# Up-projecting the last three token chunks by seven block products, in six PSUM banks

## The chip, the cores and the metric

The kernel runs on one core of a Trainium2 chip. Its engines work at the same time, each through its own queue of instructions in the order of the program: PE multiplies matrices (PEld is its loading of stationary blocks), DVE, ACT and POOL work on rows of up to 128 partitions, and SP and ACT issue transfers between the chip's memories. PE writes its results to PSUM, in which this kernel has eight banks of 128 x 512 fp32 numbers; DVE and ACT read them there. An instruction that needs another engine's result waits on a semaphore. The metric is the device time of one execution in microseconds (us); less is better.

## What is computed

The reference is attention with a sliding window followed by a two-layer network with a leaky ReLU:

```python
def _attn_ref(q, k, v):                      # (8, 8, 576, 64)
    ...
    mask_plain = (rel >= 0) & (rel < 32)
    mask_dil = (rel >= 0) & (rel < 128) & (rel % 4 == 0)
    masks = np.stack([mask_plain if h < H // 2 else mask_dil for h in range(H)], axis=0)
    ...
    return np.matmul(attn, v).astype(np.float32)

def _moe_ref(x, w_in, w_out):                # x (4608, 512), w_in (512, 2048), w_out (2048, 512)
    h = x @ w_in
    g = np.maximum(0.01 * h, h)
    return (g @ w_out).astype(np.float32)
```

The eight heads of a token, 64 numbers each, are laid side by side and make the 512 numbers of a row of x. The change is in h = x @ w_in.

## The kernel before, in words

**Tiling.** The 4608 tokens (8 batches of 576) are worked off in pairs of batches, m = 0 to 3. A pair's attention output stands transposed in `xt[m % 2]`, 128 partitions of the 512 features by 4 blocks (NI = 4) of 1152 tokens. A pair is cut into three chunks of 384 tokens, so there are 12 chunks, 0 to 11; chunks 9, 10 and 11 are those of the last pair. Within a pair each chunk is a set of columns of `xt`; `columns` (L514) gives their start and steps.

**Up-projection** (`up`, L997). The 2048 hidden numbers are 16 blocks of 128 (NJ = 16). For each chunk and each block j, four matmuls (L1014) accumulate over the features: a stationary block of `w_in` (128 x 128, every second column) against 384 moving columns of `xt`, into one of the two banks `hps`. One ACT instruction (L1025) then applies the leaky ReLU and writes the block to `gt[c % 3]` in fp16. So a chunk is 64 matmuls of 384 columns and 16 ACT instructions. One chunk of the first pair is done in two halves of 192 columns.

**Down-projection.** The first eight tiles of 128 tokens (PLAIN = 8) are projected plainly (`down`, L1055, matmuls L1066). The other 28 tiles are taken four at a time by `group` (L1105), which computes a product of 2 x 2 blocks with seven block products in place of eight: the four token tiles in two pairs are one side's blocks, and the hidden and output numbers, each cut in two, are the other's. Sums and differences of blocks of `gt` are formed by DVE (`add_up`, L1139), those of `w_out` once at about 75 us into the plan (`weight_sums`, L1091, DVE at L1095). Each product is 2 x 8 matmuls of 256 columns (L1153). Between products, ACT or DVE copies a bank's partial sums to SBUF (`evict`, L1182 and L1184), and DVE adds a bank to such a copy (`plus`, L1190). Products that build on each other accumulate in the same bank without clearing it, each after the eviction of what stood there.

A group can begin when the chunks of its tiles are up-projected. `tiles` is the list of (chunk, tile) in order, `groups` cuts it from the ninth tile on into fours. The last group is (10, 2), (11, 0), (11, 1), (11, 2) and is `split`: it uses six banks instead of two, every product is evicted in halves of 256 columns, and its results go to `v_all` and are stored half by half.

**Banks.** `sps0` and `tp` hold attention scores, the two `ops` attention outputs and transposes, the two `hps` the up-projection, the two `fps` the down-projection. The four of attention are free once the last batch's attention is done.

**Order.** All work is first entered as tasks with an engine (or a choice of engines), an assumed duration and a priority; `_Plan.run` (L85) then lays out the order of each engine's queue at build time. The order in the queue is fixed from then on: an instruction that waits holds up all behind it on its engine. `ring` (L281) hands out buffers in turn, with the users that must be done before one is reused. Priorities of the up-projection follow `begins`, 20.8 us per chunk (MOE).

**Stores** (`store`, L1049). `rows` (L1033) finds which output rows a tile's partitions belong to, in runs; each run is one transfer, issued on SP, or in the last group on SP and ACT in turn (line 263 is the helper that issues every transfer). An instruction that issues a transfer also waits until an older one, whose semaphore it takes over, has landed.

The lines by which the last group got its banks and its result buffers:

```python
            cells = [[(b, 0) for b in pair] for pair in (fps, [sps0, tpf], ops)]
            room.update({id(b): rings["S2"][-1] for b in (sps0, tpf)})
            room.update({id(b): sum(rings["O2"][-2:], []) for b in ops})
            ...
                r = (row + col) * 2 + pair[0]
                ob, o_old, o_users = v_all[:, r * HN:r * HN + HN], sum(rings["V2"][-NVS:], []), []
```

Of the kernel before, what the change touches and what calls it, by code (L numbers as in the profile page):

```python
# [11 lines left out]
AF = mybir.ActivationFunctionType  # L12
ALU = mybir.AluOpType
# [129 lines left out]
def kernel(  # L143
# [853 lines left out]
    def up(c, j, x, n, done, acc):  # L997
# [32 lines left out]
        acc[j].append((t_a, x, n))  # L1030
        return t_p

    def rows(c, tt):  # L1033

        m, i, _ = chunks[c]
        res = []
        for p in range(128):
            x = columns(c, tt * 128 + p, 1)[0]
            for b in (2 * m, 2 * m + 1):
                for u0, nu, base in segs[b]:  # L1040
                    if base <= x < base + 4 * nu:
                        tok = b * S + 4 * (u0 + (x - base) % nu) + (x - base) // nu
            if res and tok == res[-1][1] + 4 * res[-1][2]:
                res[-1][2] += 1
            else:
                res.append([p, tok, 1])
        return res

    def store(ob, i, c, tt, c0, n_o, t_c, users, both=False):  # L1049
        for n_p, (p0, tok, n) in enumerate(rows(c, tt)):  # L1050
            users.append(load("ACT" if both and n_p else "SP",
                              dram(out, tok * DM + c0, [4 * DM, n], [1, n_o]),
                              ob[p0:p0 + n, i:i + n_o], n, 4 * n_o, [t_c], -3000))

    def down(c, tt, acts, at_time):  # L1055

# [18 lines left out]
        f_users.append(t_c)  # L1075
        gt_free[c].extend(parts)
        plain_parts.extend(parts)
        store(ob, 0, c, tt, 0, DM, t_c, o_users)

    plain_parts = []  # L1080
    HJ, HN = NJ // 2, DM // 2
# [18 lines left out]
        minus(3, w_block(0, 1), w_block(1, 1), w_block(0, 1), [t_sum[1]] + plain_parts)  # L1100

    last_of = {}
    SUMS = 75.0

    def group(four, acts, at_time, split):  # L1105

# [11 lines left out]
                    for t, x, n_x in a if x < tt * 128 + 128 and x + n_x > tt * 128]  # L1118

        used = {i: [] for i in range(4)}  # L1120
        if split:
            cells = [[(b, 0) for b in pair] for pair in (fps, [sps0, tpf], ops)]
            pairs = ((0,), (1,))
            room = {id(b): last_of[id(b)] for b in fps}
            room.update({id(b): rings["S2"][-1] for b in (sps0, tpf)})
            room.update({id(b): sum(rings["O2"][-2:], []) for b in ops})
        else:
            cells = [[(b, HN * i) for i in range(2)] for b in (*fps, fps[1])]
            pairs = ((0, 1),)
            room = {id(b): last_of.get(id(b), first_banks.get(id(b), [])) for b in fps}  # L1130
# [61 lines left out]

        def result(make, deps, pair, row, col):
            if split:
                r = (row + col) * 2 + pair[0]
                ob, o_old, o_users = v_all[:, r * HN:r * HN + HN], sum(rings["V2"][-NVS:], []), []
            else:
                on, o_old = ring("OSB", NO, o_users := [])
                ob = osb[on]
            t = make(ob, deps + o_old)  # L1200
            for x, i in enumerate(pair):
                c, tt = four[row + i]
                store(ob, HN * x, c, tt, col * HN, HN, t, o_users, split)
            return t

        def kept_of(n, pair):
# [110 lines left out]
    for m in range(B // 2):  # L1317
# [97 lines left out]
```

## Time and profile before

| | |
|---|---|
| median of 3 runs | 309.73 us (309.62 to 309.89) |
| the profiled execution, its own time | 311.24 us |
| its span in the profile | 309.5 us |
| PE busy | 297.8 us, 96% of the span |
| DVE, ACT, POOL busy | 204.3, 178.7, 126.1 us |
| up-projection on PE, all 12 chunks (L1014) | 144.3 us busy, 812 matmuls recorded |
| leaky ReLU on ACT (L1025) | 93.7 us, 203 instructions |
| down-projection by groups on PE (L1153, the largest of its rows) | 53.6 us, 416 matmuls |
| share of the chain that ended last | PE 87%, DMA 4%, DVE 3%, issue of transfers on SP 3%, ACT 1% |

The span begins with the first instruction of the program and ends with its last one; the device time of that execution has a little more around it. "Busy" is the time in which an engine has an instruction under way. Matmuls overlap each other in PE's pipeline, so that the length of one is more than the time until the next one starts, and the same holds for queued instructions of DVE and ACT. The chain of work that ended last is followed back from the end: at each step to what released an instruction, or to the one before it on its engine. Lines are those of the kernel before.

### The profile page before, as it was taken

The numbers are of one execution on the slowest core, as the hardware profiler recorded it, in microseconds if no ns is written. First come the engines' busy times: TensorE is split into PE (matmuls) and PEld (weight loads), VectorE is DVE, ScalarE is ACT, GpSimd is POOL, SyncE is SP. The second block draws the span as 40 slices with busy tenths as digits, with TensorE's granted clock in tenths as the row PEclk, the third lists the DMA queues.
The fourth block names the chain that finished last, engine by engine and source line by source line (L and its number), as shares of the span: only waits on it lengthen the run. The fifth ranks groups of instructions, "written<-read, shape, count | busy, mean of one in ns | idle before, by whom it ended". The sixth has DMA issues, their size and how long they took to land.

```text
span 309.5 us, 7405 instructions
## 1 busy us (share of the span) xinstructions
PE 297.8 (96%) x2795; PEld 214.1 (69%) x2795; DVE 204.3 (66%) x419; ACT 178.7 (58%) x426; POOL 126.1 (41%) x178
## 2 busy tenths in 40 slices
PE   7987999999999999999999999999999999999993
PEld 2534645567777777787777878787887767777882
DVE  5854896689786859969798798967645230070551
ACT  3736775786556678465776665556545655445320
POOL 4449555475675639268645671961000000000000
PEclk9999999999999999999999999999999999999998
DMA  7999998999899999985999978793103010310133
GB/s 245 314 333 401 397 355 152 223 216 222 235 179 221 210 167 192 167 206 123 193 179 181 194 153 193 137 201 80 36 22 84 6 30 2 84 51 2 36 100 105
DMA packets 163188, 51.25 MB, mean 166 GB/s; under 512 B 140752, under 2 KB 160080, under 8 KB 163152
## 3 DMA queue, kind: packets, MB, share of 16 engines
q1 hardware_dynamic: 162128, 50.05, 68.1%
q10 hardware_dynamic: 1024, 0.73, 0.9%
q8 instruction: 22, 0.36, 0.5%
q14 instruction: 14, 0.11, 0.1%
HBM read 41.32 MB, written 9.44 MB: 164 GB/s over the span
## 4 chain that ended last, share of the span: by engine, by line
PE 87%; DMA 4%; DVE 3%; SPq 3%; ACT 1%; issue 1%; DVEq 0%; ACTq 0%
PE hps L1014 38%; PE fps L1153 25%; PE fps L1066 9%; PE ops L931 3%; DMA wst<-in_moe_w_in_dram 3%; SPq L263 3%; PE ops L979 2%; DVE ee L924 1%; DMA stg<-in_k_dram 1%; PE ops L1153 1%; PE tp L610 1%; PE sps L891 1%; PE tp L891 1%; PE sps L898 1%; PE tp L898 1%; ACT gt L1025 1%
## 5 line engine op out<-in xcount | busy, mean ns | idle before, releaser
L1014 PE MATMUL hps<-xt,w_in 128*128 128x384 f16 (+1 forms) x812 | 144.3, 313 | 1.4 <-DVE w_in L273 0.7
L1025 ACT ACTIVATE gt<-hps 128x384 f16<-128x384 f32 (+1 forms) x203 | 93.7, 468 | 69.9 <-PE hps L1014 67.9
L1014 PEld LDWEIGHTS <-w_in 128*128 128x128 f16 x832 | 75.2, 98 | 37.7 <-DVE w_in L273 1.5
L1153 PEld LDWEIGHTS <-gt 128*128 128x128 f16 x672 | 64.7, 98 | 12.0
L597 POOL COPY slots<-turned 64x576 f16<-64x576 f16 x48 | 35.5, 740 | 51.5 <-DVE turned L592 46.8
L1153 PE MATMUL fps<-w_out,gt 128*128 128x256 f16 x416 | 53.6, 273 | 0.0
L273 POOL CAST nat<-stg 128x576 f16<-128x576 f32 (+1 forms) x53 | 38.2, 745 | 7.5 <-DMA stg<-in_q_dram 2.7
L1066 PE MATMUL fps<-w_out,gt 128*128 128x512 f16 x128 | 32.4, 379 | 0.0
L1190 DVE TENSOR_TENSOR osb<-fps,stg 128x512 f32<-128x512 f32 x18 | 12.4, 688 | 28.0 <-ACT stg L1182 19.0
L953 DVE TENSOR_TENSOR rc<-ops,recs 96x384 f16<-96x384 f32 x48 | 25.8, 541 | 0.3
L1182 ACT COPY stg<-fps 128x512 f32<-128x512 f32 (+1 forms) x24 | 12.8, 532 | 13.2 <-PE fps L1153 11.8
L273 POOL CAST vd<-v_all 128x1024 f16<-128x1024 f32 (+2 forms) x20 | 18.0, 918 | 5.5 <-DMA v_all<-in_v_dram 5.3
L949 DVE RECIPROCAL recs<-ops 96x6 f32<-96x6 f32 x48 | 8.9, 185 | 17.2 <-PE ops L931 15.0
L924 DVE TENSOR_TENSOR ee<-ee,con 128x576 f16<-128x576 f16 x24 | 16.7, 699 | 3.8 <-ACT ee L910 3.7
L562 DVE COPY slots<-tp 64x128 f16<-64x128 f16 (+7 forms) x43 | 13.8, 334 | 8.0 <-PE tp L610 7.4
L592 DVE STREAM_TRANSPOSE turned<-nat 128x576 f16<-128x576 f16 x24 | 17.9, 755 | 0.0
L1066 PEld LDWEIGHTS <-gt 128*128 128x128 f16 x128 | 11.5, 98 | 9.1
L603 DVE STREAM_TRANSPOSE slots<-nat 128x576 f16<-128x576 f16 x24 | 17.6, 749 | 0.0
L924 DVE TENSOR_TENSOR el<-el,con 128x576 f16<-128x576 f16 x24 | 15.7, 656 | 2.1 <-ACT el L910 2.1
L273 POOL CAST vp<-v_all 128x768 f16<-128x768 f32 x16 | 15.4, 970 | 3.3 <-DMA v_all<-in_v_dram 2.1
L1139 DVE TENSOR_TENSOR gt<-gt 128x1024 f16<-128x1024 f16 x19 | 12.9, 692 | 3.8 <-PE fps L1153 3.7
L776 ACT ACTIVATE ee<-sps 128x384 f16<-128x384 f32 x20 | 9.8, 490 | 8.6 <-PE sps L770 5.7
(120 smaller groups left out, 399.6 us busy)
## 6 DMA issues: line engine op xcount, KB each, us to landing
stg<-in_q_dram SPq DMA_DIRECT2D x48, 144.0 KB, 3.8
stg<-in_k_dram SPq DMA_DIRECT2D x48, 144.0 KB, 2.9
v_all<-in_v_dram SPq DMA_DIRECT2D x24, 256.0 KB, 3.5
v_all<-in_v_dram SPq DMA_DIRECT2D x24, 192.0 KB, 2.9
gt<-in_moe_w_in_dram SPq DMA_DIRECT2D x5, 512.0 KB, 8.1
out_dram<-osb SPq DMA_DIRECT2D x24, 96.0 KB, 2.0
out_dram<-osb SPq DMA_DIRECT2D x36, 48.0 KB, 1.8
out_dram<-osb SPq DMA_DIRECT2D x25, 64.0 KB, 2.1
```

What stands on the lines that cost most here:

```text
L273: ENG[e].tensor_copy(out=dst, in_=src)
L562: nc.vector.tensor_copy(out=dst, in_=src)
L592: lambda e: nc.vector.transpose(xb, na[:, 0:S]), prio)
L597: lambda e, p0=p0, hh=hh: nc.gpsimd.tensor_copy(out=at(qb, p0, p0 + 64, hh * S + o, *od), in_=at(xb, p0, p0 + 64, i, *id_)), prio, 0.0, "m ...
L603: lambda e: nc.vector.transpose(kb[:, PAD:PAD + S], na[:, S:2 * S]), prio)
L924: nc.vector.tensor_tensor(out=x, in0=x, in1=mk, op=ALU.mult)
L953: nc.vector.tensor_tensor(out=at(xb, 0, 96, 768 * n + 64 * i, [256, 3], [128, 2], [1, D]), in0=at(ot, 0, 96, 0, [130, 3], [65, 2], [1, D]) ...
L1014: nc.tensor.matmul(ht[:, 0:n], at(w_in, 0, 128, i * DFF + j // 2 * 256 + j % 2, [2, 128]), at(xt[m % 2], 0, 128, i * 1152 + x0, *dims), st ...
L1025: lambda e: nc.scalar.activation(out=gt[c % NG][:, j * n_c + x:j * n_c + x + n], in_=ht[:, 0:n], func=AF.Prelu, alpha=0.01),
L1066: nc.tensor.matmul(ft, g[:, j * n_c + tt * 128:j * n_c + tt * 128 + 128], w_out[:, j * DM:j * DM + DM], start=(j == 0), stop=(j == NJ - 1))
L1139: lambda e: nc.vector.tensor_tensor(out=dst, in0=a, in1=b, op=op),
L1153: nc.tensor.matmul(bk[:, x:x + HN], tl[:, off + j * step:off + j * step + 128], rhs(j), start=first and x == 0 and j == 0, stop=j == HJ - ...
```

## The change

Chunks 9, 10 and 11 are up-projected by `up_fast` in place of `up`. The chunk's 384 tokens are cut in halves y of 192, the 512 features in halves k, the 2048 hidden numbers in halves h. The product of these 2 x 2 blocks is formed by seven block products. A `quarter` takes 2 of the 8 hidden blocks of 128 of each half; a chunk is four quarters. In a quarter, each product is four matmuls of 192 columns, two hidden blocks z by two feature blocks i, and fills 2 x 192 columns of a bank. Each quarter has a pair of banks X and Y: X takes products 1, 6, 5 and 3 one on top of the other, evicted after each of the first three; Y takes 2, then 7 afresh, then 4 on top of it. Three pairs are used in turn: the two `hps`, `sps0` with `tp`, and the two `ops`. Copies and sums are kept in `stg`, four tiles of three 384-column fp32 pieces. Four ACT instructions of 2 x 192 columns per quarter apply the leaky ReLU, three of them to the sums in `stg`, one to bank X, and write `gt` in the columns that `up` used too.

The operands that are sums are formed on DVE: four of `w_in` once (`w_in_sums`, 128 x 2048 fp16 each, three into the attention's `vd` tiles, the fourth in place over a block of `w_in`, after all plain projections), and four of `xt` for each chunk (`less`, 128 x 384 fp16, into a `vp` tile).

The tile (9, 2) is moved in `tiles` to the place before the last three. The last two groups become (9, 1), (10, 0), (10, 1), (10, 2) and (9, 2), (11, 0), (11, 1), (11, 2). In the last group, `sps0`, `tp` and `ops` are free when the last users of `up_ring` are done, and for the first pair of tiles both halves of a result, now side by side in `v_all`, are stored together in rows of 512 numbers: 12 stores where there were 18.

```diff
@@ -502,6 +502,7 @@
     MOE = 20.8
     PLAIN = 8
     tiles = [(c, tt) for c in range(len(chunks)) for tt in range(3)]
+    tiles.insert(-3, tiles.pop(-7))
     groups = [tiles[i:i + 4] for i in range(PLAIN, len(tiles), 4)]
     begins = [0.0]
     for m, x, n in chunks:
@@ -1030,6 +1031,138 @@
         acc[j].append((t_a, x, n))
         return t_p
 
+    plain_ups, w_in_sum, up_ring = [], {}, []
+    QJ = NJ // 2
+
+    def in_block(k, n):
+        return at(w_in, 0, 128, 2 * k * DFF + n * DFF // 2, [DFF, 2], [1, DFF // 2])
+
+    def w_in_sums():
+
+        def both(n, dst, x, y, op, deps):
+            w_in_sum[n] = add("DVE", 1.25, 0.2, deps, lambda e: nc.vector.tensor_tensor(
+                out=dst, in0=x, in1=y, op=op), IN_SUMS + n, 0.0, "T")
+
+        def home(i):
+            return at(vd[i], 0, 128, 0, [DFF // 2, 2], [1, DFF // 2])
+        v = rings["VD"]
+        last = {(len(v) - k) % NV: v[-k] for k in range(1, NV + 1)}
+        both(1, home(0), in_block(0, 1), in_block(1, 1), ALU.add, last[0])
+        both(2, home(1), home(0), in_block(0, 0), ALU.subtract, last[1] + [w_in_sum[1]])
+        both(4, home(2), in_block(1, 0), home(1), ALU.subtract, last[2] + [w_in_sum[2]])
+        both(3, in_block(0, 1), in_block(0, 0), in_block(0, 1), ALU.subtract,
+             [w_in_sum[1]] + plain_ups)
+
+    def up_fast(c, done, acc):
+
+        m, _, n_c = chunks[c]
+        n = n_c // 2
+        if not up_ring:
+            w_in_sums()
+            up_ring.append([[(hps[0], hps[1]), rings["H"][-1] + rings["H"][-2]],
+                            [(sps0, tpf), rings["S2"][-1]],
+                            [ops, rings["O2"][-1] + rings["O2"][-2]]])
+            up_ring.append([sum(rings["STG"][-NST:-1], []) + sum(rings["STG4"][1 - NST:], [])] * 4)
+        x_of = [columns(c, n * y, n)[0] for y in range(2)]
+        v = rings["VP"]
+        home, old = vp[len(v) % NV], v[-NV]
+        v.append([])
+        tx = {k: at(home, 0, 128, 2 * n * (k - 1), [n, 2], [1, n]) for k in range(1, 5)}
+        t_x = {}
+
+        def b(k, y):
+            return at(xt[m % 2], 0, 128, 2304 * k + x_of[y], [1152, 2], [1, n])
+
+        def less(k, x, y, deps):
+            t_x[k] = add("DVE", 0.08 + 2 * n * 0.00056, 0.2, deps, lambda e: nc.vector.tensor_tensor(
+                out=tx[k], in0=x, in1=y, op=ALU.subtract), begins[c] - 8, 0.0, "A")
+        less(1, b(0, 1), b(0, 0), done + old)
+        less(2, b(1, 1), tx[1], [t_x[1]])
+        less(3, b(1, 1), b(0, 1), done + old)
+        less(4, b(1, 0), tx[2], [t_x[2]])
+
+        def raw(k, h):
+            return lambda j, i: at(w_in, 0, 128, (2 * k + i) * DFF + h * DFF // 2 + j // 2 * 256 + j % 2,
+                                   [2, 128])
+
+        def summed(t):
+            return lambda j, i: at(vd[t], 0, 128, i * DFF // 2 + j // 2 * 256 + j % 2, [2, 128])
+
+        def x_raw(k, y):
+            return lambda i: at(xt[m % 2], 0, 128, (2 * k + i) * 1152 + x_of[y], [1, n])
+
+        def x_sum(k):
+            return lambda i: at(home, 0, 128, 2 * n * (k - 1) + n * i, [1, n])
+
+        w_all = sum((w_in_t[j] for j in range(NJ)), [])
+        g, g_old = gt[c % NG], gt_free.get(c - NG, [])
+
+        def quarter(p):
+            bank_of = up_ring[0].pop(0)
+            (X, Y), room = bank_of
+            room_k = up_ring[1].pop(0)
+            kn = (4 * (c - FAST[0]) + p) % 4
+            keep = [stg[kn][:, 2 * n * z:2 * n * z + 2 * n] for z in range(3)]
+            when = begins[c] + p * 4.6 - (0.0, 2.0, 7.0)[c - FAST[0]]
+
+            def product(k, lhs, rhs, cell, first, deps):
+                def pe(e):
+                    for z in range(2):
+                        for i in range(2):
+                            nc.tensor.matmul(cell[:, n * z:n * z + n], lhs(2 * p + z, i), rhs(i),
+                                             start=first and z == 0 and i == 0,
+                                             stop=z == 1 and i == 1, skip_group_check=True)
+                return add("PE", 0.33, 0.25, deps, pe, when + 0.6 * k, 0.0, "U")
+
+            def evict(z, deps):
+                dst = keep[z]
+
...
+                return add((("ACT", 0.5), ("DVE", 0.55)), None,
+                           0.22, deps, fn, -1000 + c * 16, 0.0, "C")
+
+            def plus(z, deps):
+                return add("DVE", 0.09 + 2 * n * 0.00115, 0.25, deps, lambda e: nc.vector.tensor_tensor(
+                    out=keep[z], in0=Y[:, 0:2 * n], in1=keep[z], op=ALU.add), -1000 + c * 16, 0.0, "C")
+
+            def relu(src, row, y, deps):
+                j = row * QJ + 2 * p
+                t = add("ACT", 0.45, 0.22, deps + g_old,
+                        lambda e: nc.scalar.activation(
+                            out=at(g, 0, 128, j * n_c + n * y, [n_c, 2], [1, n]),
+                            in_=at(src, 0, 128, 0, [n, 2], [1, n]), func=AF.Prelu, alpha=0.01),
+                        -1000 + c * 16 + p)
+                for z in range(2):
+                    acc[j + z].append((t, n * y, n))
+                return t
+
+            p1 = product(0, raw(0, 0), x_raw(0, 0), X, True, done + w_all + room)
+            p2 = product(1, raw(1, 0), x_raw(1, 0), Y, True, done + w_all + room)
+            e1 = evict(0, [p1] + room_k)
+            a11 = plus(0, [e1, p2])
+            r11 = relu(keep[0], 0, 0, [a11])
+            p6 = product(2, summed(1), x_sum(2), X, False, [e1, t_x[2], w_in_sum[2]])
+            p7 = product(3, raw(0, 1), x_sum(3), Y, True, [a11, t_x[3], w_in_sum[3]])
+            e2 = evict(1, [p6] + room_k)
+            p5 = product(4, summed(0), x_sum(1), X, False, [e2, t_x[1], w_in_sum[1]])
+            e4 = evict(2, [p5] + room_k)
+            a22 = plus(2, [e4, p7])
+            r22 = relu(keep[2], 1, 1, [a22])
+            p3 = product(5, summed(2), x_raw(1, 1), X, False, [e4, w_in_sum[4]])
+            p4 = product(6, raw(1, 1), x_sum(4), Y, False, [a22, t_x[4]])
+            r12 = relu(X[:, 0:2 * n], 0, 1, [p3])
+            a21 = plus(1, [e2, p4])
+            r21 = relu(keep[1], 1, 0, [a21])
+            up_ring[0].append([bank_of[0], [r12, a21]])
+            up_ring[1].append([r11, r22, r21])
+
+        for p in range(QJ // 2):
+            quarter(p)
+
     def rows(c, tt):
 
         m, i, _ = chunks[c]
...
@@ -1100,7 +1233,8 @@
         minus(3, w_block(0, 1), w_block(1, 1), w_block(0, 1), [t_sum[1]] + plain_parts)
 
     last_of = {}
-    SUMS = 75.0
+    SUMS, IN_SUMS = 75.0, 190.0
+    FAST = (9, 10, 11)
 
     def group(four, acts, at_time, split):
 
@@ -1118,12 +1252,13 @@
                     for t, x, n_x in a if x < tt * 128 + 128 and x + n_x > tt * 128]
 
         used = {i: [] for i in range(4)}
+        whole = {i: [] for i in range(4)}
         if split:
             cells = [[(b, 0) for b in pair] for pair in (fps, [sps0, tpf], ops)]
             pairs = ((0,), (1,))
             room = {id(b): last_of[id(b)] for b in fps}
-            room.update({id(b): rings["S2"][-1] for b in (sps0, tpf)})
-            room.update({id(b): sum(rings["O2"][-2:], []) for b in ops})
+            for pair, users in up_ring[0]:
+                room.update({id(b): users for b in pair})
         else:
             cells = [[(b, HN * i) for i in range(2)] for b in (*fps, fps[1])]
             pairs = ((0, 1),)
@@ -1192,15 +1327,23 @@
 
         def result(make, deps, pair, row, col):
             if split:
-                r = (row + col) * 2 + pair[0]
-                ob, o_old, o_users = v_all[:, r * HN:r * HN + HN], sum(rings["V2"][-NVS:], []), []
+                r = 2 * (row + pair[0]) + col
+                ob, o_old = v_all[:, r * HN:r * HN + HN], sum(rings["V2"][-NVS:], [])
+                t = make(ob, deps + o_old)
+                whole[row + pair[0]].append(t)
+                at_once = len(whole[row + pair[0]]) if row == 0 else 1
+                if row or at_once == 2:
+                    c, tt = four[row + pair[0]]
+                    store(v_all, r * HN - (at_once - 1) * HN, c, tt, (col + 1 - at_once) * HN,
+                          at_once * HN, whole[row + pair[0]][-at_once:], [], True)
+                return t
             else:
                 on, o_old = ring("OSB", NO, o_users := [])
                 ob = osb[on]
             t = make(ob, deps + o_old)
             for x, i in enumerate(pair):
                 c, tt = four[row + i]
-                store(ob, HN * x, c, tt, col * HN, HN, t, o_users, split)
+                store(ob, HN * x, c, tt, col * HN, HN, [t], o_users)
             return t
 
         def kept_of(n, pair):
@@ -1333,8 +1476,12 @@
             acts = first_acts if n_c == 0 else [[] for _ in range(NJ)]
             halves = [(0, 192), (192, 192)] if m == 0 and n_c % 3 == 2 else [(0, 384)]
             for i, (x, n) in enumerate(halves):
-                x_free[m + 2] += [up(n_c, j, x, n, x_done[n_c, i], acts)
-                                 for j in range(0 if n_c else N_UPS, NJ)]
+                if n_c in FAST:
+                    up_fast(n_c, x_done[n_c, i], acts)
+                    continue
+                plain_ups += [up(n_c, j, x, n, x_done[n_c, i], acts)
+                              for j in range(0 if n_c else N_UPS, NJ)]
+                x_free[m + 2] += plain_ups[-(NJ if n_c else NJ - N_UPS):]
             gt_free[n_c] = []
             all_acts[n_c] = acts
             for i, (c, tt) in enumerate(tiles[:PLAIN]):
```

More of the change, by code (lines that the diff above doesn't have):

```diff
@@ new lines, in up_fast, with fn @@
+    def up_fast(c, done, acc):
[50 more added lines that the diff above has]
+                dst = keep[z]
+                def fn(e):
+                    if e == "ACT":
+                        nc.scalar.copy(out=dst, in_=X[:, 0:2 * n])
+                    else:
+                        nc.vector.tensor_copy(out=dst, in_=X[:, 0:2 * n])
+                return add((("ACT", 0.5), ("DVE", 0.55)), None,
[34 more added lines that the diff above has]
+            quarter(p)
@@ L1052, in store @@
                               dram(out, tok * DM + c0, [4 * DM, n], [1, n_o]),
-                              ob[p0:p0 + n, i:i + n_o], n, 4 * n_o, [t_c], -3000))
+                              ob[p0:p0 + n, i:i + n_o], n, 4 * n_o, t_c, -3000))
     def down(c, tt, acts, at_time):
@@ L1077, in down @@
         plain_parts.extend(parts)
-        store(ob, 0, c, tt, 0, DM, t_c, o_users)
+        store(ob, 0, c, tt, 0, DM, [t_c], o_users)
     plain_parts = []
```

## The prediction

> **What bounds the kernel now.** First the page: the engines' busy shares, and the span in 40 slices.
>
> ```profile
> PE 297.8 (96%) x2795; PEld 214.1 (69%) x2795; DVE 204.3 (66%) x419; ACT 178.7 (58%) x426; POOL 126.1 (41%) x178
> ...
> PE   7987999999999999999999999999999999999993
> ```
>
> PE is full from the fourth slice to the last. Then four stretches of the end: length, busy us and count of PE, PEld, DVE, ACT and POOL, granted clock, DMA share, GB/s.
>
> ```profile
> 247.00:265.00 18.00, 18.00 (x136) 13.02 (x134) 3.46 (x5) 9.14 (x19) 0.00 (x0) 1.00 0.11 30
> 265.00:289.50 24.50, 24.50 (x183) 17.75 (x182) 6.94 (x11) 12.35 (x26) 0.00 (x0) 1.00 0.13 34
> 289.50:304.20 14.70, 14.70 (x136) 13.01 (x133) 8.08 (x16) 3.66 (x9) 0.00 (x0) 1.00 0.36 100
> 304.20:309.50 5.30, 0.09 (x1) 0.00 (x0) 0.42 (x1) 0.00 (x0) 0.00 (x0) 0.82 0.26 74
> ```
>
> While the last chunks are projected, PE never waits, DVE has a quarter of the time, ACT half. So the end comes when PE has worked off its matmuls, and 5.3 us of stores and closing follow. What counts is PE's time per matmul, in the timeline of PE (start, length, count):
>
> ```profile
> 98.66 0.82 PE L1014 MATMUL hps<-xt,w_in 128*128 128x192 f16 x8
> 99.32 1.03 PE L1066 MATMUL fps<-w_out,gt 128*128 128x512 f16 x4
> ...
> 103.43 1.46 PE L1014 MATMUL hps<-xt,w_in 128*128 128x384 f16 x8
> 104.73 1.03 PE L1066 MATMUL fps<-w_out,gt 128*128 128x512 f16 x4
> ```
>
> From a group's start to the next, 8 matmuls of 192 columns take 0.66 us, 82 ns each, and 8 of 384 take 1.30 us, 162 ns each. Both load a weight block for every matmul.
>
> **PE's own work.** Each of three chunks loses 16 x 4 matmuls of 384 columns: 192 x 162 ns = 31.1 us. It gets 4 quarters x 7 products x 4 matmuls of 192: 336 x 82 ns = 27.55 us. That is -3.55 us; down-projections and attention have the same matmuls as before, in another order. The w_in_sums operands are read with the same step-2 columns as w_in, so I take 82 ns for them too.
>
> A rule speaks against this. The Trainium skill, "TensorE: Matmul & The Clock Gate", section "Back-to-back issue gap", says that in a real stream of weight loads and matmuls the spacing is about 81 ns at 128 columns and 131 ns at 512. A line between them gives, as an estimate, 89 ns at 192 and 114 ns at 384: 29.9 us against 21.9 us, a loss of 8 us. The rows above are of this very line and pattern, so they decide.
>
> **What ACT and DVE get.** Per quarter 3 evictions of 384 columns (X to SBUF), 3 sums of PSUM and SBUF, and 4 activations where there were 4. Prices: first the groups of instructions by shape (busy, mean ns of one), then, from the timelines of ACT and DVE, how closely queued ones follow each other.
>
> ```profile
> L1025 ACT ACTIVATE gt<-hps 128x384 f16<-128x384 f32 x55 | 27.0, 491 | 23.4 <-PE hps L1014 22.9
> L1190 DVE TENSOR_TENSOR osb<-fps,stg 128x512 f32<-128x512 f32 x8 | 5.5, 692 | 24.8 <-ACT stg L1182 18.3 <-PE fps L1153 6.5
> ...
> L1190 DVE TENSOR_TENSOR v_all<-ops,stg 128x256 f32<-128x256 f32 x4 | 1.7, 425 | 3.9 <-ACT stg L1182 3.0 <-PE ops L1153 0.9
> ```
>
> ```profile
> 228.70 0.49 ACT L1025 ACTIVATE gt<-hps 128x384 f16<-128x384 f32 x1
> 229.09 0.41 ACT L910 ACTIVATE ee<-sps 128x288 f16<-128x288 f32 x1
> ...
> 294.72 0.69 DVE L1139 TENSOR_TENSOR gt<-rest,gt 128x1024 f16<-128x1024 f16 x1 [1.06 <-PE fps L1153]
> 295.33 0.42 DVE L1190 TENSOR_TENSOR v_all<-sps,stg 128x256 f32<-128x256 f32 x1
> 295.67 0.68 DVE L1139 TENSOR_TENSOR gt<-pair,gt 128x1024 f16<-128x1024 f16 x1
> ```
>
> A queued ACT instruction of 0.49 us is followed after 0.39; on DVE 0.69 is followed after 0.61 and 0.42 after 0.34. An ACT copy of 384 columns lies between 0.37 (256) and 0.585 (512): 0.48. A DVE sum of 384 lies between 0.425 and 0.69: 0.56, followed after 0.475.
>
> Queue loads. By the built program's order, from the first block product to the last there are 84 products and 21 down products of 8 x 109 ns: 46.5 us on PE. On ACT: 26 evictions and 48 activations at 0.39, 6 copies of 512 columns at 0.48 and one of 0.54: 32 us. On DVE: 46 evictions and sums at 0.475, 20 of 0.61, 8 of 0.27, the fourth weight sum at 1.14 and 1.3 us of attention: 38.7 us. Both fit, but not evenly. In the middle, where 31 products stand among 3 down products, PE has 12.8 us, ACT 27 instructions or 10.6 us, DVE 18 sums and evictions, 5 of 0.61 and 6 of 0.27: 13.2 us. DVE is full there, and its last three (1.6 us) may finish later, since no product waits for them.
>
> Links. In the tail, 8 matmuls of ops begun at 302.38 give way at 303.25 and DVE starts at 303.46: 0.21 us. In the chain of waits an early PE start at 23.08 follows DVE's end at 23.04; I take 0.05. So product, eviction, next product on the bank is 0.21 + 0.48 + 0.05 = 0.74 us by ACT, 0.82 by DVE. In the dense places the program puts at least three products of 0.33 between: 0.99 us. Following the three queues by hand in the program's order with these rows, I find no later product that waits, with margins of 0.25 us at the closest.
>
> One wait is left, at the beginning. The second matmul of the first product waits for the fourth weight sum, which overwrites a w_in block after the last plain projection. That is 0.21 + 1.22 (L1095 took 1.22 at this size) + 0.05 = 1.48 us after that projection; PE has 0.87 + 0.08 us of other work: a stall of 0.5. Everything on PE stands behind it; on DVE the mask of the last attention unit and the first evictions do, which come in time. The other three weight sums and the subtractions (3.7 + 1 us) fall between 215 and 237 us, where DVE is about half idle and POOL done: nothing. If that cover were gone, each would delay a mask for the value products, 1.2 us at worst.
>
> Stalls in all: 0.5 at least; 2.0 if ACT's instructions did not overlap (I followed the queues that way too). I take 0.7, nearer to the overlapped rows.
>
> **The tail.** Before, the last results end at 303.88 and 304.75, but the stores wait for older ones, whose semaphores they reuse (timeline; the last line is of the queues' table for 303 to 305):
>
> ```profile
> 303.41 3.23 ACTq L263 DMA_DIRECT2D out_dram<-v_all  x3
> 304.33 0.42 DVE L1190 TENSOR_TENSOR v_all<-ops,stg 128x256 f32<-128x256 f32 x1 [0.45 <-PE ops L1153]
> 305.69 1.23 SPq L263 DMA_DIRECT2D out_dram<-v_all  x2
> ...
> q8 instruction: 1, 0.02, 3.2%
> ```
>
> SP issues at 305.69 and 306.25 what was ready at 303.88 and 304.75. An instruction fetch holds one DMA engine for 3.2% x 16 x 2 = 1.02 us in that moment. After: 12 stores instead of 18, 6 on each queue, of the same bytes; c11 is stored with c12 in rows of 2 KB, so 256 KB move from about 296 into the last 4 us. PE has 288 more instructions and one fetch per 256, so the fetch comes some 16 matmuls, 1.7 us, earlier before the end. If nothing waits, the last store goes at 304.8 instead of 306.25: -1.45. If the added 256 KB lie in the way at the 100 to 200 GB/s seen there, they cost up to 1.3 to 2.6, and the saving is gone: +0.5 at worst. I take -0.9, nearer to the first, as fewer stores share the eight semaphores.
>
> **Sum.** The profiled execution took 311.24 us, of which its span is 309.5. Span: 309.5 - 3.55 + 0.7 - 0.9 = 305.75. The runs' median is 309.73, so 309.73 - 3.75 = 306.0 us.
>
> **Rivals.**
> A, the forecast: 305.2 to 307.0 (stall 0.5 to 1.2, tail -1.45 to -0.4). Chance 0.56.
> B, the links bind: in-order queues make some products wait, 2 to 4.5 us in all. For it: DVE at 13.2 of 12.8 us in the middle. Against: margins of 0.25 us. With 2.5: 307.8; from about 3.9 it is no change. Chance 0.20, of which 0.03 no change.
> C, the stretch holds but the stores still wait: tail 0 to +0.5, 306.9 to 307.4. For it: the moved 256 KB. Chance 0.09.
> D, slower: DVE's and ACT's instructions do not follow closely, because each waits for the one before it through a bank. Then DVE needs 18 x 0.58 + 5 x 0.7 + 6 x 0.35 = 16.0 us in the middle, 3.2 over PE, and 46.5 us in the whole, with no time left to wait. I put 6 us on it: 309.73 - 3.55 + 6 - 0.9 = 311.3. It decides from 5.1 us of stall, 0.42 per quarter. Against: the closely queued rows. Chance 0.13.
> E, the change doesn't make PE's work smaller: weight loads (98 ns each in the profile) set the pace of 192 columns. Then 336 x 16 ns = 5.4 us come back: 311.4. Against: 82 ns above, with such loads. Chance 0.02.
>
> Runs before lie within 0.27 us, so 0.2% (0.6 us) is about what can be told. Faster: 0.56 + 0.17 + 0.09 = 0.82; within 0.2%: 0.03; slower: 0.13 + 0.02 = 0.15. The range reaches from 0.2 (the runs' spread) under A's lower end to B with 3.7 us of stall: 305.0 to 309.0.
>
> **What would show it.** The 192-column products 82 ns apart; PE idle 0.5 us before the first product's second matmul, released by DVE's in-place w_in sum, and hardly anywhere after; PE's last matmul at 301.3 on the span's clock; 4.4 us from there to the end of the span. Wrong, if L1112's matmuls show idle time ended by ACT or DVE of several us, or if stores again start over 1 us after their results.

## The result, and the profile after

The changed kernel takes 306.43 us (median of 4 runs, 306.35 to 306.96) where the one before takes 309.81 (4 runs, 309.62 to 311.07): ratio 0.9886, 95% interval 0.9857 to 0.9914, or 3.4 us less. Forecast were 306.0 us and 3.75 less. A second measurement of the same kernel, on another chip, gave 306.36 against 310.26, ratio 0.9859 (0.9822 to 0.9896).

The two profiled executions differ by more: 311.24 and 306.96 us, spans 309.5 and 305.2. First the page of the kernel after, its busy times and PE's row of the 40 slices; then its table of stretches with the columns shown before (length, busy us and count of PE, PEld, DVE, ACT, POOL, granted clock, DMA share, GB/s).

```profile
PE 294.3 (96%) x2939; PEld 223.0 (73%) x2939; DVE 234.8 (77%) x481; ACT 187.0 (61%) x452; POOL 126.1 (41%) x178
...
PE   7887989999999999999999999999999999999994
```

```profile
236.00:247.00 11.00, 10.96 (x133) 10.37 (x131) 9.74 (x19) 7.62 (x18) 0.00 (x0) 1.00 0.10 25
247.00:260.00 13.00, 13.00 (x151) 12.67 (x149) 12.35 (x28) 11.54 (x29) 0.00 (x0) 1.00 0.09 23
260.00:283.00 23.00, 23.00 (x244) 21.72 (x243) 17.48 (x33) 16.35 (x37) 0.00 (x0) 1.00 0.18 47
283.00:301.00 18.00, 18.00 (x170) 16.20 (x168) 9.27 (x17) 4.93 (x12) 0.00 (x0) 1.00 0.26 71
```

The row to look at is 247 to 260: DVE works 12.35 of 13.0 us and ACT 11.54, and PE still has work in every moment. PE did 144 matmuls more in less time, and remains what sets the end.

The difference of the two spans divides into three parts, read from the starts of PE's recorded matmuls: up to a common point in the first third (the 61st recorded matmul of the up-projection into the banks `hps`), from there to the start of PE's last matmul, and from there to the end of the span.

| profiled execution | common point at | to PE's last matmul | tail | sum = span |
|---|---|---|---|---|
| before | 58.68 | 245.34 | 5.43 | 309.45 |
| after | 59.26 | 241.81 | 4.10 | 305.18 |
| difference | +0.58 | -3.53 | -1.33 | -4.28 |

The first part is not of the change, which comes later in the program: up to 208 us PE does the same matmuls in the same order. It is time in which PE waits for what is loaded and converted at the start, and it differs from execution to execution. The two waits that grew most, before (L1014, L814) and after (L1015, L815; columns: us in all, times, longest):

```profile
PE hps L1014 <- DVE w_in L273: 0.7, 2, 0.5
...
PE ops L814 <- POOL vd L273: 0.5, 1, 0.5
```

```profile
PE hps L1015 <- DVE w_in L273: 1.2, 2, 1.0
...
PE ops L815 <- POOL vd L273: 0.9, 1, 0.9
```

Other waits of the start shrank: one of 0.6 us before, for `slots`, has no match after. In the 12 profiles that follow, the common point lies anywhere from 57.6 to 59.4 us. So a single time says little below 1 us, and the parts of a trace say more.

### The profile page after: what moved, and what is told of

Same layout as the page of the kernel before. It is cut to its first block, busy times and chain, and to the rows that moved or that the text cites. A ratio compares the mean times of both kernels' runs of the same rounds, so it can differ in the third digit from the quotient of the medians.

```text
span 305.2 us, 7803 instructions
## 1 busy us (share of the span) xinstructions
PE 294.3 (96%) x2939; PEld 223.0 (73%) x2939; DVE 234.8 (77%) x481; ACT 187.0 (61%) x452; POOL 126.1 (41%) x178
## 4 chain that ended last, share of the span: by engine, by line
PE 85%; DMA 4%; DVE 3%; SPq 3%; ACT 2%; issue 1%; DVEq 0%; ACTq 0%
PE hps L1015 28%; PE fps L1288 25%; PE fps L1199 9%; PE ops L932 3%; DMA wst<-in_moe_w_in_dram 3%; PE hps L1112 3%; PE ops L1112 3%; SPq L263 3%; PE ops L980 2%; PE sps L1112 2%; PE tp L1112 1%; DVE ee L925 1%; DMA stg<-in_k_dram 1%; PE ops L1288 1%; ACT gt L1026 1%; PE sps L892 1%
## 5 line engine op out<-in xcount | busy, mean ns | idle before, releaser
L1015 PE MATMUL hps<-xt,w_in 128*128 128x384 f16 (+1 forms) x620 | 109.0, 309 | 1.4 <-DVE w_in L273 1.2
L1026 ACT ACTIVATE gt<-hps 128x384 f16<-128x384 f32 (+1 forms) x155 | 70.2, 461 | 51.7 <-PE hps L1015 50.2
L1015 PEld LDWEIGHTS <-w_in 128*128 128x128 f16 x640 | 56.6, 98 | 27.5 <-DVE w_in L273 2.0
L1317 ACT COPY stg<-fps 128x512 f32<-128x512 f32 (+1 forms) x24 | 12.8, 533 | 12.1 <-PE fps L1288 12.0
L1135 ACT ACTIVATE gt<-stg 128x384 f16<-128x384 f32 x36 | 18.0, 524 | 1.1 <-DVE stg L1129 1.1
L925 DVE TENSOR_TENSOR el<-el,con 128x576 f16<-128x576 f16 x24 | 14.8, 615 | 2.8 <-ACT el L911 2.7
L1112 PEld LDWEIGHTS <-w_in 128*128 128x128 f16 x192 | 16.4, 98 | 0.5 <-DVE w_in L1043 0.3
```

The lines of the kernel that those rows point to most:

```text
L925: nc.vector.tensor_tensor(out=x, in0=x, in1=mk, op=ALU.mult)
L1015: nc.tensor.matmul(ht[:, 0:n], at(w_in, 0, 128, i * DFF + j // 2 * 256 + j % 2, [2, 128]), at(xt[m % 2], 0, 128, i * 1152 + x0, *dims), st ...
L1026: lambda e: nc.scalar.activation(out=gt[c % NG][:, j * n_c + x:j * n_c + x + n], in_=ht[:, 0:n], func=AF.Prelu, alpha=0.01),
L1112: nc.tensor.matmul(cell[:, n * z:n * z + n], lhs(2 * p + z, i), rhs(i), start=first and z == 0 and i == 0, stop=z == 1 and i == 1, skip_gr ...
L1135: lambda e: nc.scalar.activation(out=at(g, 0, 128, j * n_c + n * y, [n_c, 2], [1, n]), in_=at(src, 0, 128, 0, [n, 2], [1, n]), func=AF.Pre ...
```

## Experiments

All are compared with the kernel before, run on the same chip between them. Three groups of four ran, on three chips. "Stores" counts the transfers of the last group's results, from `v_all`. "Fetch" is how far the last instruction fetch of the 16 KB kind (queue q8) starts ahead of PE's last matmul. These fetches are taken to be PE's: there are 22 before for PE's 5590 matmuls and loads and 23 after for 5878, one for some 255. Stretch and tail are the second and third part above. The last four columns are of the profiled execution.

| kernel | median us (before) | ratio, 95% interval | stretch | stores | fetch | tail |
|---|---|---|---|---|---|---|
| before, profile shown | 309.73 | 1 | 245.3 | 18 | 0.7 | 5.4 |
| after, profile shown | 306.43 (309.81) | 0.9886 (0.9857 to 0.9914) | 241.8 | 12 | 3.6 | 4.1 |
| plain_up | 310.33 (310.22) | 1.0011 (0.9989 to 1.0032) | 245.3 | 12 | 1.6 | 5.1 |
| old_stores | 305.65 (310.22) | 0.9877 (0.9852 to 0.9902) | 241.4 | 16 | 3.7 | 3.6 |
| two_chunks | 309.01 (310.22) | 0.9952 (0.9930 to 0.9974) | 243.6 | 12 | 12.8 | 4.1 |
| plain_order | 306.37 (310.22) | 0.9882 (0.9860 to 0.9903) | 242.2 | 13 | 3.0 | 4.1 |
| after_again | 306.36 (310.26) | 0.9859 (0.9822 to 0.9896) | 241.4 | 12 | 3.5 | 4.0 |
| split_old | 306.83 (310.26) | 0.9894 (0.9854 to 0.9933) | 241.4 | 16 | 2.8 | 4.5 |
| before_early | 309.10 (310.26) | 0.9951 (0.9928 to 0.9973) | 246.1 | 18 | 4.5 | 3.6 |
| after_late | 306.19 (310.26) | 0.9880 (0.9832 to 0.9929) | 241.6 | 12 | none in 15 us | 3.9 |
| dve_plus1 | 306.66 (309.80) | 0.9878 (0.9848 to 0.9908) | 242.0 | 12 | 3.6 | 3.9 |
| dve_plus3 | 314.09 (309.80) | 1.0118 (1.0091 to 1.0146) | 249.4 | 12 | 3.6 | 4.0 |
| act_plus3 | 315.56 (309.80) | 1.0169 (1.0138 to 1.0200) | 251.1 | 12 | 2.7 | 4.3 |
| after_early | 305.97 (309.80) | 0.9862 (0.9831 to 0.9893) | 241.4 | 12 | 6.7 | 3.9 |

### What each part of the change is worth

**plain_up**: `FAST = ()`, and the last group's banks from the attention's rings as before.

```diff
-    FAST = (9, 10, 11)
+    FAST = ()
...
-            for pair, users in up_ring[0]:
-                room.update({id(b): users for b in pair})
+            room.update({id(b): rings["S2"][-1] for b in (sps0, tpf)})
+            room.update({id(b): sum(rings["O2"][-2:], []) for b in ops})
```

> The three chunks are up-projected as before (plain products of 384 columns); the new tile order and the 12 merged stores stay. Theory 1, the PE term is the whole difference: 31.1 us of products come back for 27.55 and the 0.2 us wait goes, so 306.43 + 3.35 = 309.8 us, no different from the kernel before, and the merged stores are worth nothing outside the profiled execution. Theory 2, the stores are worth the 1.3 us by which the two profiled tails differ: 309.81 - 1.3 = 308.5 us. Theory 3, the tail was shortened because the instruction fetch came earlier before the end: with 288 PE instructions fewer it falls back to about 0.8 us before PE's end, and the tail in this trace is 5 us and not 4.

No difference from before can be measured. PE's stretch is that of before (245.3), so the fast up-projection is the whole 3.5 us of it. With 288 PE instructions fewer the fetch stands near the end again, and the tail is 5.1 us in spite of 12 stores: theories 1 and 3 hold.

**old_stores**: each result of the last group stored by itself again.

```diff
-                whole[row + pair[0]].append(t)
-                at_once = len(whole[row + pair[0]]) if row == 0 else 1
-                if row or at_once == 2:
-                    c, tt = four[row + pair[0]]
-                    store(v_all, r * HN - (at_once - 1) * HN, c, tt, (col + 1 - at_once) * HN,
-                          at_once * HN, whole[row + pair[0]][-at_once:], [], True)
+                c, tt = four[row + pair[0]]
+                store(v_all, r * HN, c, tt, col * HN, HN, [t], [], True)
```

> The fast up-projection and the tile order stay; each result of the last group is stored by itself again, 18 stores and not 12. Theory 1, the number of stores sets the tail (they wait for semaphores of older ones): 306.43 + 0.9 to 1.4 = 307.3 to 307.8 us, and the last stores start over 1 us after their results. Theory 2, the position of the instruction fetch made the difference: it still comes 3.7 us before PE's end, so the tail stays at 4.0 us and the time at 306.4 to 306.7.

16 stores, and a tail of 3.6 us. (Not 18: with the new order of tiles the rows of the last group fall into one run less, and each run was stored twice.) Theory 1 falls: the number of stores is not what made the tail short.

**two_chunks**: `FAST = (10, 11)`.

> Only the last two chunks are projected by seven products; chunk 9 in plain ones. Theory 1, PE's time counts and every chunk gives the same: 64 x 162 ns - 112 x 82 ns = 1.18 us, so 306.43 + 1.2 = 307.6 us. Theory 2, the chunk that shares the last attention units gains less, since DVE and ACT have less room there: 306.4 to 307.0.

Both theories missed: 307.6 us was the most that was expected. PE's stretch is 1.76 us longer than after's, of which 1.2 is the arithmetic and the rest waits of this kernel's own order: behind an ACT eviction at 285 a matmul starts 0.5 us late (0.3 of it idle), and the fourth weight sum, at 252, costs 0.1 more than after. By the medians chunk 9 is worth more, about 2.6 us against after's two measurements. Of the remaining 0.8, some 0.4 lies outside the profiled span: the executions of this kernel take 2.1 to 2.2 us more than their spans, those of plain_order on the same chip 1.8. The rest, a start that differs or something of its own, stays open.

**plain_order**: without `tiles.insert(-3, tiles.pop(-7))`.

> The tile order alone is undone: the last group holds a tile of chunk 10 and not of chunk 9. Theory 1, the order of tiles moves no work that PE waits for: 306.43 +- 0.2. Theory 2, the last group's sums of gt come later and PE waits for DVE between the last products: 0.5 us or more, to be seen as idle time of L1288's matmuls in the last 20 us.

306.37 us: the order of tiles, and the one store that it saves, are worth nothing that can be measured. PE has one wait more, at 288: it is idle for 0.17 us, and the next matmul starts 0.33 us late. That is the direction of theory 2, but less than its 0.5 us.

### What the tail hangs on

**before_early**: the kernel before, with other warm-up matmuls.

```diff
-    for i in range(8):
-        add("PE", 0.43, 0.0, [t_warm],
-            lambda e: nc.tensor.matmul(fps[0], warm[:, 0:128], zeros(512), start=True, stop=True),
+    for i in range(32):
+        add("PE", 0.1075, 0.0, [t_warm],
+            lambda e: nc.tensor.matmul(fps[0][:, 0:128], warm[:, 0:128], zeros(128), start=True, stop=True),
```

> The kernel before, with its 8 warm-up matmuls of 512 columns cut into 32 of 128: the same columns, 24 more matmuls, so that every later instruction fetch comes 24 matmuls or 2.6 us earlier, the last one 3.4 us ahead of PE's end and not 0.8. Theory 1, the fetch's place set the tail of before: tail 4.1 us and not 5.1 to 5.4, and the time 1.0 to 1.3 us below before in these runs. Theory 2, it does so in profiled executions only: the tail in the trace is 4.1, the time 0 to 0.3 below. Theory 3, the stores' semaphores set it: 5.1 to 5.4 as before, time unchanged.

Nothing else is altered, and the tail is 3.6 us where it was 5.4; the median is 1.2 us below before's, ratio 0.9951. In the profiled execution the common point comes 0.8 us earlier, but PE loses that again between 207 and 211, where it waits for operands of the attention that come no earlier (from its waits; us in all, times, longest):

```profile
PE ops L931 <- DVE el L924: 1.1, 2, 0.9
```

So PE's last matmul starts at 304.01 where it started at 304.02 before, and the whole difference of the two spans (307.62 and 309.45) is the tail. Compare the tails: the fetch in the queues' table for the 2 or 3 us around it (packets, MB, share of 16 engines), and the timelines' rows of the last DVE result and the last stores (start, length). First plain_up, fetch between 302 and 305:

```profile
q8 instruction: 1, 0.02, 3.4%
```

```profile
303.22 1.38 SPq L263 DMA_DIRECT2D out_dram<-v_all  x1
...
304.51 0.42 DVE L1325 TENSOR_TENSOR v_all<-ops,stg 128x256 f32<-128x256 f32 x1 [0.45 <-PE ops L1288]
...
305.94 0.64 SPq L263 DMA_DIRECT2D out_dram<-v_all  x1
```

Then before_early, fetch between 299 and 301:

```profile
q8 instruction: 1, 0.02, 2.7%
```

```profile
304.31 0.42 DVE L1190 TENSOR_TENSOR v_all<-ops,stg 128x256 f32<-128x256 f32 x1 [0.45 <-PE ops L1153]
304.77 0.49 ACTq L263 DMA_DIRECT2D out_dram<-v_all  x1
```

And after, fetch between 297 and 299:

```profile
q8 instruction: 1, 0.02, 3.1%
```

```profile
301.39 0.42 DVE L1325 TENSOR_TENSOR v_all<-ops,stg 128x256 f32<-128x256 f32 x1 [0.45 <-PE ops L1288]
...
301.84 0.32 SPq L263 DMA_DIRECT2D out_dram<-v_all  x1
301.85 0.50 ACTq L263 DMA_DIRECT2D out_dram<-v_all  x1
```

With the fetch among the last stores, SP issues the last one at 305.94, 1.0 us after its result (304.51 + 0.42); with the fetch 3.6 us ahead or more it goes 0.03 to 0.04 us after it, with 18 stores or with 12. The fetch lasts 3.4% x 16 x 3 = 1.6 us in plain_up and 0.9 in before_early. By the same table, plain_up's stores issued at that time took 2.6 to 4.6 us to land, those of after's last 6 us 2.0 to 2.7.

The traces show the delay itself. The landing of a store is recorded in 16 parts. Four stores that before and before_early issue at the same time, to 0.03 us (start of issue before; landing of the 15th and 16th part, us):

| issued | before: 15th | 16th | before_early: 15th | 16th |
|---|---|---|---|---|
| 300.97, ACT | 303.42 | 305.45 | 303.40 | 303.42 |
| 301.75, SP | 303.59 | 305.62 | 303.58 | 303.59 |
| 301.84, ACT | 303.81 | 305.80 | 303.82 | 303.82 |
| 302.16, SP | 303.99 | 305.98 | 303.97 | 304.00 |

Before, one part in 16 of each is 2.0 us late, with the fetch under way from 303.34 to 304.36; in before_early, whose fetch lies at 299.5, none of these is. The four stores that take over the semaphores of these are issued 0.07 to 0.3 us after the late parts land, at 305.52, 305.69, 306.10 and 306.25. So the late sixteenth parts hold up the last stores. That each late part stood behind the fetch on the same DMA engine is the reading that fits, as the records do not name the engine; why it is late by 2.0 us where the fetch lasts 1.0 is open.

**after_early**: the changed kernel with the same warm-up matmuls, as a control.

> The changed kernel with the same 32 short warm-up matmuls that moved the fetch in the kernel before by 24 matmuls. Here the last fetch is already 3.6 us ahead of PE's end, and goes to about 6. Theory 1, those warm-up matmuls saved 1.16 us there through the fetch in the tail: here nothing, tail 3.6 to 4.1 us, time that of the changed kernel (306.4). Theory 2, they saved it at the start: here the same 0.8 to 1.2 us, 305.4.

305.97 us, ratio 0.9862, where the changed kernel had 0.9859 and 0.9886: no gain that can be told, though intervals of 0.3% either way could hide one below 1 us. With the tails above, this leaves the fetch's place as the cause: 1.8 us in the profiled execution, 1.2 us by the medians.

**after_late**: the changed kernel with a longer warm-up loop.

```diff
-    for i in range(8):
-        add("PE", 0.43, 0.0, [t_warm],
-            lambda e: nc.tensor.matmul(fps[0], warm[:, 0:128], zeros(512), start=True, stop=True),
+    for i in range(109):
+        add("PE", 0.0316, 0.0, [t_warm],
+            lambda e: nc.tensor.matmul(fps[0][:, 0:32], warm[:, 0:128], warm[:, 0:32], start=True, stop=True),
```

> The changed kernel with 109 short warm-up matmuls of 32 columns in place of 8 of 512, 101 more matmuls: the last fetch moves back from 3.75 us to about 0.8 us ahead of PE's end. Theory 1: the tail in the trace grows from 4.1 to 5.1 - 5.4 us with the same 12 stores, and some of the last stores start over 1 us after their results. Theory 2, the stores' number set it: 4.1. The time is not read here, since the start may be longer by 1 to 3 us (PE's clock rises later).

A miss: the fetch did not come late but not at all in the last 15 us before PE's end. The tail of 3.9 us is in line with the rest, and tells nothing apart.

### The wait for the fourth weight sum

**split_old**: old_stores, and the sum cut into its two blocks of features.

```diff
-        both(3, in_block(0, 1), in_block(0, 0), in_block(0, 1), ALU.subtract,
-             [w_in_sum[1]] + plain_ups)
+        for i in range(2):
+            a, z = (w_in[:, i * DFF + x:i * DFF + x + DFF // 2] for x in (0, DFF // 2))
+            w_in_sum[3 + 2 * i] = add("DVE", 0.65, 0.2, [w_in_sum[1]] + plain_ups,
...
-            p7 = product(3, raw(0, 1), x_sum(3), Y, True, [a11, t_x[3], w_in_sum[3]])
+            p7 = product(3, raw(0, 1), x_sum(3), Y, True, [a11, t_x[3], w_in_sum[3], w_in_sum[5]])
```

> 18 stores as before, and the fourth sum of w_in in two halves, one for each block of 128 rows, so that the first product no longer waits for it. If the reading of that wait is right (it reaches over rows the first product does not share), the idle 0.2 us before its second matmul is gone: 305.65 - 0.2 = 305.4 us, 0.9 below the changed kernel in the same group. If the wait moves to the fourth product, which does read the block, 0.2 us stay there: 305.65.

In the timeline of PE the first four matmuls of the first product (L1112, here L1116) take 0.71 us after and 0.49 here:

```profile
236.75 0.71 PE L1112 MATMUL sps<-xt,w_in 128*128 128x192 f16 x4
```

```profile
236.08 0.49 PE L1116 MATMUL sps<-xt,w_in 128*128 128x192 f16 x4
```

The wait is gone and did not move. The first product reads the first halves of two blocks of features and the sum writes their second halves, so no number is shared; the reading that fits is that the one instruction counts as one range of addresses, which encloses the first half of the second block. The 0.2 us cannot be found in the time: 306.83 against after_again's 306.36, with overlapping intervals, where 305.4 was expected. Nor is it in the stretch, 241.4 us here and in old_stores. The tail, 4.5 us, is longer than old_stores' 3.6, with the fetch 0.9 us nearer to the end. No version that beats the changed kernel by a measurable amount came out of these runs.

### How much room DVE and ACT had left

**dve_plus1** and **dve_plus3** add 1 and 3 copies per quarter, **act_plus3** three on ACT (behind the last `relu`). The copies go to a buffer that has no further use. The edits of dve_plus3 and act_plus3 (dve_plus1 has 1 in place of 3):

```diff
             def plus(z, deps):
+                def fn(e):
+                    nc.vector.tensor_tensor(out=keep[z], in0=Y[:, 0:2 * n], in1=keep[z], op=ALU.add)
+                    for _ in range(3 * (z == 1)):
+                        nc.vector.tensor_copy(out=nat[0].bitcast(FP32)[:, 0:384], in_=keep[z])
...
             def relu(src, row, y, deps):
...
+                    for _ in range(3 * (row == 1 and y == 0)):
+                        nc.scalar.copy(out=nat[1].bitcast(FP32)[:, 0:384], in_=keep[1])
```

> The changed kernel with one more DVE instruction per quarter, 12 in all, behind the quarter's last sum: a copy of 384 columns that nobody waits for (0.25 to 0.45 us each). Where the products stand closest (247 to 260 us) DVE worked 12.35 of 13.0 us. Theory 1, DVE's load decides: it gets 4.4 x 0.35 = 1.5 us more there, 0.9 over what is free, so PE loses about 0.9 us, nothing elsewhere. Theory 2, each link decides and has 0.25 us of margin: 12 x 0.1 = 1.2 us, spread over all quarters. Theory 3, there is more room than the busy shares tell: 0.

> The same with three such copies per quarter, 36 in all. Theory 1 (load): 4.4 x 1.05 = 4.6 us more in the dense stretch, 4 over what is free: PE loses about 4 us there, and little elsewhere. Theory 2 (links): 12 x (1.05 - 0.25) = 9.6 us over all quarters. In both the gain of the change is gone, the time 310 to 316 us; theory 3: under 1 us.

> The changed kernel with three more ACT copies of 384 columns per quarter behind the quarter's last activation (0.39 us each where they follow closely). ACT worked 11.54 of 13.0 us in the dense stretch. Theory 1 (load): 4.4 x 1.2 = 5.3 us more, 3.8 over what is free: PE loses about 3.8 us there. Theory 2 (links): 12 x (1.2 - 0.25) = 11 us over all quarters.

The stretch from 247 to 260 of dve_plus1, then two of dve_plus3:

```profile
247.00:260.00 13.00, 13.00 (x150) 12.55 (x148) 12.86 (x31) 11.60 (x28) 0.00 (x0) 1.00 0.09 23
```

```profile
247.00:260.00 13.00, 11.36 (x125) 10.65 (x125) 12.76 (x31) 9.23 (x22) 0.00 (x0) 1.00 0.08 21
260.00:267.00 7.00, 5.41 (x57) 4.87 (x56) 6.72 (x17) 5.23 (x12) 0.00 (x0) 1.00 0.01 2
```

Twelve copies of 0.36 us, 4.3 in all, cost nothing: DVE is 99% busy in the dense stretch and PE does not wait. What does not fit there is done between 260 and 283, where DVE works 17.48 of 23 us in the changed kernel and 19.79 here. Theory 3 holds. With three copies, which follow each other after 0.395 us (1.18 us per quarter), PE waits in eight places, mostly for banks that DVE has not freed, and its stretch grows by 7.6 us; from PE's waits between 236 and 300:

```profile
PE hps L1112 <- DVE stg L1124: 1.7, 2, 1.4
PE ops L1112 <- DVE stg L1130: 1.7, 2, 1.0
PE tp L1112 <- DVE stg L1130: 1.6, 2, 1.2
```

Per quarter that is 1.18 us put in and 0.63 lost, so by the difference about 0.55 us were free. On ACT three copies follow each other after 0.54 us, and the next instruction starts 1.50 us after the first: about 1.5 us per quarter. The stretch grows by 9.3 us, 0.77 per quarter, so about 0.7 were free. The size lies between the two theories, nearer to the links: once the queue is full, an eviction behind the copies holds PE up, and not only in the dense stretch.

## Why the prediction was right, and where it was not

**PE's own work: right.** -3.55 us was forecast for the matmuls, and the stretch shrank by 3.53 with the stall in it (by 3.9 in after_again). The 192-column matmuls start 82 ns apart: eight of them take 0.82 us, of which the last one's length is 0.25.

```profile
237.29 0.82 PE L1112 MATMUL hps<-xt,w_in 128*128 128x192 f16 x8
```

The rule of the Trainium skill, "TensorE: Matmul & The Clock Gate", "Back-to-back issue gap", which by an estimate made a loss of 8 us of it, does not hold here. Rival E is gone with it: the loads of 98 ns overlap and set no pace (mean ns behind the bar, then the one wait).

```profile
L1112 PEld LDWEIGHTS <-w_in 128*128 128x128 f16 x192 | 16.4, 98 | 0.5 <-DVE w_in L1043 0.3
```

**Loads of DVE and ACT: right, with more margin than thought.** The taken prices were met, by groups of instructions (busy, mean ns): 0.56 us for the sum of 384 columns, 0.48 for ACT's copy.

```profile
L1129 DVE TENSOR_TENSOR stg<-hps,stg 128x384 f32<-128x384 f32 x12 | 6.6, 552 | 0.5 <-PE hps L1112 0.4
...
L1122 ACT COPY stg<-ops 128x384 f32<-128x384 f32 x10 | 4.8, 480 | 3.8 <-PE ops L1112 3.5
```

"DVE is full there" was right too (12.35 of 13 us). But full did not mean late: rivals B (stalls of 2 to 4.5 us) and D, to which 0.33 was given, needed a queue that runs behind. For D's slower result a stall of 0.42 us per quarter was said to be the point; the runs put 0.55 us of spare DVE time per quarter in front of it. Those 0.55 us are what remains of one experiment's difference, so an estimate; that one copy per quarter cost nothing agrees with it. The margin could not be read off the busy shares. The "0.25 us at the closest" of the hand-made queues was a lower one.

**The stall: right place, 0.2 us and not 0.5.** The sum was taken to start 0.21 us after the last plain projection's end. It starts before that end: in the timelines below, PE's last four matmuls of that projection begin at 235.22, the last of them at 235.71, and DVE begins at 235.75.

```profile
235.22 0.81 PE L1015 MATMUL hps<-xt,w_in 128*128 128x384 f16 x4
```

```profile
235.75 1.23 DVE L1043 TENSOR_TENSOR w_in<-w_in 128x2048 f16<-128x2048 f16 x1 [0.54 <-PE hps L1015]
```

Only the first two of the four read rows of the overwritten block, so it waits for the second, which signals its end at 235.73 and starts 0.33 us before the fourth: 0.5 - 0.33 is the 0.2 seen. The mistake was to let the wait end with the whole projection. No other product waited, so the taken 0.7 was 0.5 too much.

**The tail: about the right size, half the wrong reason.** -0.9 was forecast, -1.3 is in the profiles. The prediction gave two causes: fewer stores that share semaphores, and a fetch that comes earlier. old_stores and plain_up show that the first is worth nothing: 16 stores with an early fetch have the short tail, 12 with a late one the long. If anything the merged stores end later: with the fetch 3 us ahead or more, the tail is 3.6 us in old_stores and before_early and 3.9 to 4.1 in the kernels with 12 or 13 stores. before_early shows that the second does it alone. "The fetch comes some 16 matmuls, 1.7 us, earlier before the end" was too little: it went from 0.7 to 3.6 us, and why by 2.9 is not shown. Rival C (stores still wait because 256 KB were moved late) did not happen.

**The sum.** The profiled executions differ by -4.28 us, the parts of their spans by +0.58 - 3.53 - 1.33. The medians differ by -3.4 and -3.9 in two measurements. Of this PE's part is 3.5 to 3.9 by the profiles, and the fetch's place 1.2 where it was measured by itself; together they are more than the medians show. Starts that vary by 1.8 us between executions hide how much of the tail's gain reaches the median. So it is partly luck that the medians lie within 0.4 us of the forecast 3.75: stretch and tail together shrank by 4.9 us in the profiles, 1.1 more than forecast, since the stall was taken too large and the tail's gain too small.

## What to carry to other kernels

Price a block-product scheme by the measured spacing of matmuls of the new width, and then ask how long evictions may be late, not how busy their engine is: here DVE at 99% cost nothing, and 0.8 us more per quarter cost 7.4 us. When a kernel ends in a row of small stores, look where the last instruction fetch falls, since a few more or fewer PE instructions move it. Before giving a gain at the end to the edit that was made there, run that edit alone.

## What was not expected of the hardware

A fetch of 16 KB, 1.0 us long, cost the kernel before 1.2 us because it fell among the last stores: one part in 16 of four stores landed 2.0 us late. The Trainium skill, "Runtime: NRT & Kernel Launch", "Instruction fetch mechanics", says that crossing a 16 KB boundary is mostly hidden. For PE this case agrees: from 59 us on its longest wait before is 0.2 us, for DVE. The sentence does not speak of the transfers around a fetch, and these were held up here. And 101 more instruction pairs at the start did not move the last fetch to the place counted, 0.8 us ahead of PE's end, but out of the stretch: the places can be counted from one kernel to the next only roughly.
